# The last sparse tile's values in a buffer of their own, loaded about 15 ticks earlier

## The chip, the cores and the metric

One core of one Trainium2 chip runs the whole program. The metric is the device time of one execution in microseconds; the kernel before took 523.57 us (median of 3 runs, 522.68 to 530.19).

## The reference

Block-sparse attention over 4 batches, 8 heads, 768 positions, head size 64, in blocks of 32; its output rows (3072 tokens of 512 numbers) go through a mixture of 8 experts, of which each token uses one. All in float32.

```python
scores = scale * np.matmul(q, k.transpose(0, 1, 3, 2))
mask = np.abs(blk_i - blk_j) <= window            # window = 1
mask = mask | (blk_i == 0) | (blk_j == 0) | (blk_i == n_blocks - 1) | (blk_j == n_blocks - 1)
for qb in range(n_blocks):
    for kb in sampled_blocks[qb]:                 # 3 sampled blocks for each query block
        mask[qb * block:(qb + 1) * block, kb * block:(kb + 1) * block] = True
attn = softmax(np.where(mask, scores, -1e9)); x = np.matmul(attn, v)
e_idx = np.argmax(x @ w_gate + modality_bias[modality_id], axis=1)
h = np.maximum(x[e_idx == e] @ w1[e], 0.0)        # w1[e]: 512 x 1024, w2[e]: 1024 x 512
out[e_idx == e] = gate_w * (h @ w2[e])
```

## The kernel before, in words

**Attention.** The first and last query blocks attend to everything (dense items). The other 22 blocks of each half of the batch go two at a time: a sparse tile `g` of 22 (`2 * NM`; 11 in each half, `g = half * NM + m`) holds 128 rows. Its keys lie in `kbuf[g % 2]` and its values in `vbuf[g % 2]`, a tile of 128 partitions x 3 columns x 1024: column 1 holds the blocks that both query blocks use (first and last block, put there once in each half's first two tiles and left, and two neighbours), columns 0 and 2 those that one of the two uses alone. `fetch_v` (L509) loads two row blocks of column 1 or 2 (2 DMAs of 128 KB; 4 more where the half begins), `share_v` (L531) copies two row blocks from the tile before on POOL, `fetch_own` (L548) loads the sampled blocks (3 DMAs of 128 KB in each of two calls). All loads are issued from SP's queue, in program order.

**Ticks.** There are 104 items (`NI`): 16 dense ones and 88 sparse ones, four to a tile. The order of the work on every engine is written out: at tick `t` each operation `op` of `ORDER` is done for item `t - LAG[kind][op]`: S scores, M mask and maximum, X exponentials, T transposes (L590), A copies (L595), W `weigh_shared` (L612, products with column 1), V `sum_rows` and `weigh_own` (L605, L621, products with columns 0 and 2), O division, Y transposes of the rows (L628), G gate (L638). Between operations, `hook(place)` runs what `side(t, f, place)` has put there. Tile 19's last item is at tick 95, tile 20's at 99, tile 21's (the last) at 103. W of tile 20 is at tick 104 and V at 106; W of tile 21 at 108 and V at 110. By `VL` and `VG`, tile 19's values are loaded at ticks 95, 96 and 97, tile 20's at 99, 100 and 101, tile 21's at 103, 104 and 105.

**The start of the experts.** `early_groups` (L859) is stepped once a tick, and twice from tick 104 on, beside the end of the attention. It begins at tick 91, so its own count `tick` is 0 there, 12 at tick 103, 19 and 20 at tick 107, 21 and 22 at 108, 23 and 24 at 109. With each of its steps `load` issues half a weight fetch (256 KB, L749) or one `split`: a cast of 128x1024 weights on ACT (L760), whose remainder `low` (L763) is taken on the next step on DVE. `TICKS` (6, 9, 12) says from which count the first, second and third split are due. `staged` gives the first eight weight tiles two staging buffers in turn (a third for the last of them), so weight tile n+2 is fetched after split n. `rows(0)` gathers the token rows of the first expert group (2 indirect DMAs on POOL, L774) once `share_v` of the last tile is issued; 9 steps later `columns(0)` transposes them (L805, two steps of 4 transposes) and casts them (ACT L811, DVE L812). From tick 111 (`tail[0]`) the first products `up` (L818 to L820) of group 0 follow, then `down` (L833 to L835), then group 1, and after the attention's end groups in a loop. Group 1's rows are gathered once `tail[1]` is set, into slot 8, which is the buffer of the odd tiles' values.

**Buffers.** `slot(n)` allocates one of ten tiles; a new allocation of the same slot waits for the last reader of the old one. Slots 0 to 3 and 9 hold dense keys and values, 5 and 6 `kbuf`, 7 and 8 `vbuf`. `expert_slots` takes slots over for the experts: slot 0 (the first batch's keys) and 2 for weights at tick 111.

Of the kernel before, what the change touches and what calls it, by code (L numbers as in the profile page):

```python
# [10 lines left out]
F32R = mybir.dt.float32r  # L11
# [28 lines left out]
NM = NB // 2 - 1  # L40
# [29 lines left out]
VL = (8, 1)  # L70
VS = (11, 7)
VS_SOON = (8, 7)
VG = ((9, 6), (10, 3))

DENSE_IN = ((19, 14, 30), (49, 38, 44))
Q_IN = 22
# [4 lines left out]
EVAC_DVE = ()  # L81
POOL_SPLITS = (7, 15, 16, 21)

TICKS = (6, 9, 12)
DOWN0 = ((9, 5), (9, 7), (14, 7), (12, 9), (13, 9), (13, 9), (17, 9), (15, 10))
UP1 = ((13, 8), (13, 14), (17, 15), (20, 15))
DOWN1 = ((16, 17), (17, 16), (17, 17), (23, 18), (21, 17), (23, 18), (23, 19), (22, 19))
# [3 lines left out]
def attention_moe(ctx, tc, kD, qD, qH, v0, v1, blocks, modality, w_gate, bias, w1, w2, out):  # L91
# [30 lines left out]
    with ExitStack() as actx:  # L122
# [9 lines left out]
        def slot(n, dt=F32):  # L132
            return big.tile([P, 3 * 1024 + 2], dt, name="slot", tag=f"slot{n}", bufs=1)
# [5 lines left out]
        ad = [ad[:, 768 * n:768 * n + 768].rearrange("p (k f) -> p k f", k=6) for n in range(4)]  # L139
        kbuf = [slot(5 + n)[:, 0:3072].rearrange("p (s f) -> p s f", s=12) for n in range(2)]  # L140
        vbuf = [slot(7 + n)[:, 0:3072].rearrange("p (c f) -> p c f", c=3) for n in range(2)]
        qd = {}

        def fetch_q(half, m):
# [363 lines left out]

        def fetch_v(m, half):  # L509
            i, g = 2 * m + 1, half * NM + m  # L510
            vg = vbuf[g % 2]

            def rows_in(r, c, j):
                nc.sync.dma_start(vg[r, c, :].rearrange("p (b f) -> p b f", b=HB), vblock(half, j))

            if m < 2:
                for n, j in ((0, 0), (1, NB - 1)):
                    rows_in(slice(32 + 32 * n, 64 + 32 * n), 1, j)
            if m == 0:
                for n in range(2):  # L520
                    rows_in(slice(0, 32), 1 + n, i + 2 * n)
                for n in range(2):
                    rows_in(slice(96, P), n, i - 1 + 2 * n)
                return
            rows_in(slice(0, 32), 2, i + 2)
            rows_in(slice(96, P), 1, i + 1)
# [4 lines left out]
        def share_v(m, half):  # L531
            g = half * NM + m
            shared.append(g)
            new, old = vbuf[g % 2], vbuf[(g - 1) % 2]
            for r, c in ((slice(96, P), 0), (slice(0, 32), 1)):
                nc.gpsimd.tensor_scalar(new[r, c, :], old[r, c + 1, :], 1.0, 1.0, ALU.mult, ALU.mult)  # L536
            g = max(picked) + 1
            if g < 2 * NM:
                key_numbers(g)
# [7 lines left out]

        def fetch_own(m, half, n):  # L548
            i, g = 2 * m + 1, half * NM + m
            vg = vbuf[g % 2]  # L550
            for k in ((0, 2, 1), (2, 0, 1))[n]:
                reg = own[g][3 * n + k]
                nc.sync.dma_start(vg[32 * (k + n):32 * (k + n) + 32, 2 * n, :].rearrange("p (b f) -> p b f", b=HB), vblock(half, reg))
# [51 lines left out]
                nc.tensor.matmul(tp[32 * j:32 * j + 32, 0:H], lhsT=fold, rhs=r[:, j], start=True, stop=True, tile_position=(0, 32 * j))  # L605

        def weigh_shared(g, o, a):
            vg = vbuf[g % 2]
            for h in range(H):
                pr, u = divmod(h, 2)  # L610
                for b in range(HB):
                    nc.tensor.matmul(o[64 * b:64 * b + 64, D * h:D * h + D], lhsT=a[b][:, 8 * u + 4 + pr].rearrange("p n q -> p (n q)"),  # L612
                                     rhs=vg[:, 1, b * HD + D * h:b * HD + D * h + D], start=h == 0, stop=False, tile_position=(0, 64 * b))

        def weigh_own(g, o, a):
            vg = vbuf[g % 2]
            for h in range(H):
                pr, u = divmod(h, 2)
                for j in range(4):
                    b, n = divmod(j, 2)  # L620
                    nc.tensor.matmul(o[32 * j:32 * j + 32, D * h:D * h + D], lhsT=a[b][:, 8 * u + pr, n],  # L621
                                     rhs=vg[:, 2 * n, b * HD + D * h:b * HD + D * h + D], start=False, stop=h == H - 1, tile_position=(0, 32 * j))
# [61 lines left out]
        def pieces(n, dt, *sizes):  # L684
            t, k = slot(n, dt), 0
            for size in sizes:
                yield t[:, k:k + size]
                k += size
# [5 lines left out]
        def expert_slots(*ns):  # L694
            cols_ = lambda ap: ap.rearrange("p (c t) -> p c t", t=GT)
            W, X, Y = 1024, HD, HD + 1
            for n in ns:
                if n == 0:
                    w = [*pieces(1, F32R, W, W, W), *pieces(3, F32R, W, W, W)]
                    wh[:], wl[:] = w[0::2], w[1::2]  # L700
                    wx = list(pieces(9, F32R, W, W))
                    xh.append(cols_(wx[0]))
                    xl.append(cols_(wx[1]))
                    a = list(pieces(4, F32, W, W, 2 * Y))
                    stg.extend(a[0:2])
                    rows_in(a[2])
                elif n == 2:
                    w = [*pieces(0, F32R, W, W, W), *pieces(2, F32R, W)]
                    wh.extend(w[0::2])
                    wl.extend(w[1::2])  # L710
                elif n == 5:
                    a = list(pieces(5, F32R, 2 * W, W))
                    hh.append(cols_(a[0]))
                    hl.append(cols_(a[1]))
                elif n == 6:
                    a = list(pieces(6, F32R, W, W, W))
                    hl.append(cols_(a[0]))
                    xh.append(cols_(a[1]))
                    xl.append(cols_(a[2]))
                elif n == 7:  # L720
                    stg.extend(pieces(7, F32, W, W, W))
                elif n == 8:
                    a = list(pieces(8, F32, 2 * Y, X, X, W))
                    rows_in(a[0])
                    og.extend(a[1:3])
                    xq.append(a[3])
# [132 lines left out]
        def early_groups():  # L859
# [39 lines left out]
            while not tail[0]:  # L899
                while lows:  # L900
                    lows.pop()()
                rows(0)
                if now["gather"]:
                    wait += 1
                    if wait > 8:
                        columns(0)
                p = sum(tick >= x for x in TICKS)
                load(p + 2, p, True)
                tick += 1
                yield "tick"  # L910
            while lows:
                lows.pop()()
            expert_slots(2, 5, 6, 7)
            while now["column"] < 2:
                rows(0)
                columns(0)
# [350 lines left out]
        def side(t, f, place=7):  # L1267
            work_at.setdefault((t, place), []).append(f)
# [58 lines left out]
        for g in range(2 * NM):  # L1327
            half, m = divmod(g, NM)
            t = at["s", half, m, 0, 0]
            kl = lambda m=m, half=half: q_load(m, half)  # L1330
            qp = lambda m=m, half=half: share_k(m, half)
            vl = lambda m=m, half=half: fetch_v(m, half)
            vg = [lambda m=m, half=half, n=n: fetch_own(m, half, n) for n in range(2)]
            if g < 2:
                loads.update({f"kl{g}": kl, f"qp{g}": qp, f"vl{g}": vl, "vs1": lambda: share_v(1, 0), **{f"v{n}{g}": vg[n] for n in range(2)}})
                continue
            kt = last(g - 2) + KL[0]
            pt = max(kt, t + QP[0])
            vt = last(g - 2) + VL[0]
            side(kt, kl, KL[1])  # L1340
            side(pt, qp, QP[1])
            side(vt, vl, VL[1])
            if m:
                vs = VS_SOON if g >= 2 * NM - 2 else VS
                side(last(g - 2) + vs[0], lambda m=m, half=half: share_v(m, half), vs[1])
            for n in range(2):
                side(last(g - 2) + VG[n][0], vg[n], VG[n][1])

        st, done = {}, set()

# [68 lines left out]
        with man:  # L1419
# [16 lines left out]
            while t < NI + LAG["s"]["G"] + 1 or fillers or slots_todo or choosers or early:  # L1436
                spot = 0
                for op in ORDER:
                    if op in "TSMAXOW":
                        hook(spot)  # L1440
                        spot += 1
                    for kind in "ds":
                        k = t - LAG[kind][op]
                        if 0 <= k < NI and items[k][0] == kind:
                            do(op, items[k])
                hook(7)
                if t >= NI:
                    tail[0], tail[1] = t >= NI + TAIL, t >= NI + LAG["s"]["V"]
                    for _ in range(2):
                        advance(2)  # L1450
                        while slots_todo:
                            slot_lhs(nc.vector if len(slots_todo) % 2 else nc.gpsimd)
                        step(choosers, 1)
                        step(early, 1)
                t += 1
# [61 lines left out]
```

## Time and profile before

| what | us |
|---|---|
| median of 3 runs (range) | 523.57 (522.68 to 530.19) |
| the profiled execution: its time, its span | 527.1, 525.4 |
| PE busy | 501.7 (95%) |
| DVE busy | 386.4 (74%) |
| ACT busy | 336.0 (64%) |
| POOL busy | 248.1 (47%) |
| mean granted TensorE clock | 0.993 |

The profile is one execution on the core. PE is the matmul engine, PEld its weight loads, DVE, ACT and POOL the vector, scalar and GpSimd engines, SP the engine whose queue issues the loads. Idle time before an instruction stands in square brackets with what seems to have ended it. The clock is a share of 2.4 GHz: 1.00 is that level, 0.50 the lower one of 1.2 GHz.

### The profile page before, as it was taken

Reading aid. Unit: us, or ns where it says so; the run is one execution under the profiler, and the core shown is the slowest. Engines: PE = TensorE matmul, PEld = TensorE weight load, DVE = VectorE, ACT = ScalarE, POOL = GpSimd, SP = SyncE. Lnnn points to the kernel's source line nnn. Section 1 sums busy time; section 2 is a strip of 40 time slices with the busy share of each in tenths; the row PEclk is TensorE's granted clock in tenths of the full one; section 3 lists DMA queues with packets and bytes.
Section 4 is the critical chain, followed back from the end, with each engine's and each line's share of the span. In section 5 each row is a group of like instructions: output and inputs, shape, how many; then the busy total and the mean of one; then the engine's idle time right before and its main releaser. Section 6 shows DMA issues by size and latency. Waiting matters only on the chain.

```text
span 525.4 us, 18967 instructions
## 1 busy us (share of the span) xinstructions
PE 501.7 (95%) x7124; PEld 423.3 (81%) x7124; DVE 386.4 (74%) x1136; ACT 336.0 (64%) x765; POOL 248.1 (47%) x514
## 2 busy tenths in 40 slices
PE   7999989979999999789999999999999999999995
PEld 5677767767877867688898898988989899898984
DVE  6886678676689899756986768676686767768673
ACT  4798877978879889634444556555565555555562
POOL 6789675567458983310455241423224222342423
PEclk9999999999999999979999999999999999999999
DMA  8976997899657778946778797969688786867860
GB/s 295 311 218 200 250 254 207 233 246 258 206 165 200 198 214 248 252 123 226 256 237 298 243 310 265 273 223 307 207 260 249 247 283 201 293 199 260 263 225 24
DMA packets 65143, 123.84 MB, mean 236 GB/s; under 512 B 9745, under 2 KB 17682, under 8 KB 65042
## 3 DMA queue, kind: packets, MB, share of 16 engines
q1 hardware_dynamic: 60784, 108.88, 68.2%
q0 software_dynamic: 4256, 13.65, 7.6%
q8 instruction: 58, 0.95, 0.8%
q14 instruction: 43, 0.35, 0.3%
q10 hardware_dynamic: 2, 0.00, 0.0%
HBM read 105.97 MB, written 12.86 MB: 226 GB/s over the span
## 4 chain that ended last, share of the span: by engine, by line
PE 69%; DMA 13%; DVE 10%; issue 3%; SPq 3%; ACT 1%; POOL 1%; DVEq 0%; POOLq 0%; ACTq 0%
PE bank L818 7%; PE bank L819 7%; PE bank L820 7%; DMA slot<-x_d,gi 7%; PE bank L565 6%; PE bank L590 6%; PE bank L834 6%; PE bank L835 6%; PE bank L833 6%; PE bank L612 4%; PE bank L621 3%; DMA slot<-w 3%; PE bank L451 2%; DMA slot<-v 2%; PE bank L638 2%
## 5 line engine op out<-in xcount | busy, mean ns | idle before, releaser
L763 DVE TENSOR_TENSOR slot<-slot 128x1024 fp32r<-128x1024 f32 x99 | 124.7, 1272 | 62.4 <-ACT slot L760 52.6
L760 ACT CAST slot<-slot 128x1024 fp32r<-128x1024 f32 x104 | 107.1, 1047 | 67.2 <-PE bank L819 45.2
L818 PE MATMUL bank<-slot 128*128 128x256 f32 x384 | 108.5, 283 | 0.0
L820 PE MATMUL bank<-slot 128*128 128x256 f32 x384 | 107.8, 281 | 0.0
L819 PE MATMUL bank<-slot 128*128 128x256 f32 x384 | 107.6, 280 | 0.0
L581 ACT ACTIVATE a<-y,mn 128x256 f32<-128x256 f32 x176 | 88.5, 510 | 7.6 <-DVE mn L573 6.8
L854 POOL DMA_INDIRECT out<-slot,si x20 | 27.4, 1369 | 105.7 <-ACT slot L850 102.7
L834 PE MATMUL bank<-slot 128*128 128x512 f32 x192 | 75.9, 395 | 0.0
L833 PE MATMUL bank<-slot 128*128 128x512 f32 x192 | 75.8, 395 | 0.0
L835 PE MATMUL bank<-slot 128*128 128x512 f32 x192 | 75.7, 394 | 0.0
L818 PEld LDWEIGHTS bank<-slot 128*128 128x128 f32 x384 | 72.4, 188 | 0.7 <-ACT slot L760 0.2
L819 PEld LDWEIGHTS bank<-slot 128*128 128x128 f32 x384 | 72.3, 188 | 0.4
L820 PEld LDWEIGHTS bank<-slot 128*128 128x128 f32 x384 | 72.2, 188 | 0.0
L573 DVE CUSTOM_DVE_ANT_1 y<-bank,smask 128x256 f32<-128x256 f32 x176 | 66.2, 416 | 0.3
L502 POOL COPY slot<-slot 128x128 f32 x264 | 64.0, 296 | 0.0
L536 POOL TENSOR_SCALAR slot<-slot 32x1024 f32<-32x1024 f32 x40 | 41.9, 1047 | 33.1 <-PE bank L621 16.8
L595 ACT COPY at<-bank 128x512 f32<-128x512 f32 x88 | 50.6, 576 | 9.8 <-PE bank L590 9.8
L590 PE MATMUL bank<-ident,a 128*128 128x128 f32 x352 | 52.1, 280 | 2.5 <-DVE rt L459 1.6
L565 PE MATMUL bank<-slot,q_raw 64*32 64x256 f32 x1408 | 48.4, 382 | 0.0
L590 PEld LDWEIGHTS bank<-ident,a 128*128 128x128 f32 x352 | 38.1, 141 | 6.9 <-issue 1.7
L835 PEld LDWEIGHTS bank<-slot 128*128 128x128 f32 x192 | 36.1, 188 | 8.5 <-issue 0.2
L834 PEld LDWEIGHTS bank<-slot 128*128 128x128 f32 x192 | 36.0, 188 | 8.3 <-DVE slot L763 0.4
(307 smaller groups left out, 865.5 us busy)
## 6 DMA issues: line engine op xcount, KB each, us to landing
slot<-w SPq DMA_DIRECT2D x100, 512.0 KB
slot<-v SPq DMA_DIRECT2D x188, 128.0 KB
x_d<-xr SPq DMA_DIRECT2D x22, 256.5 KB
q_raw<-qH SPq DMA_DIRECT2D x22, 256.0 KB
slot<-slot SPq DMA_DIRECT2D x120, 32.0 KB
slot<-kD SPq DMA_DIRECT2D x13, 256.0 KB
slot<-v SPq DMA_DIRECT2D x4, 768.0 KB
slot<-v SPq DMA_DIRECT2D x12, 256.0 KB
```

The lines of the kernel that those rows point to most:

```text
L565: nc.tensor.matmul(sp[u][32 * pr:32 * pr + 32, b * 256:(b + 1) * 256], lhsT=q[r, b * NPAIR + pr, n, :], rhs=kv[r, s0:s0 + 8, b, pr, :], st ...
L573: nc.vector.tensor_tensor_reduce(y[:, u, :].rearrange("p (s f) -> p s f", s=8), sp[u][:, b * 256:(b + 1) * 256].rearrange("p (s f) -> p s ...
L581: nc.scalar.activation(a[:, u, :], y[:, u, :], AF.Exp, bias=mn[:, u:u + 1], scale=-1.0, accum_out=total[:, u:u + 1])
L590: nc.tensor.transpose(tp[:, k:k + P], a[:, u, c * P:(c + 1) * P], ident)
L760: nc.scalar.copy(h, s)
L763: (eng or (nc.gpsimd if n in POOL_SPLITS else nc.vector)).tensor_tensor(l, s, h.bitcast(F32), ALU.subtract)
L818: nc.tensor.matmul(o, lhsT=h[:, fs], rhs=xh[g % 2][:, c, :], start=c == 0 and f % 2 == 0, stop=False)
L819: nc.tensor.matmul(o, lhsT=h[:, fs], rhs=xl[g % 2][:, c, :], start=False, stop=False)
L820: nc.tensor.matmul(o, lhsT=l[:, fs], rhs=xh[g % 2][:, c, :], start=False, stop=c == 3 and f % 2 == 1)
L833: nc.tensor.matmul(o, lhsT=hh[0][:, f, ts_], rhs=h[:, fs], start=f == 0, stop=False)
L834: nc.tensor.matmul(o, lhsT=hh[0][:, f, ts_], rhs=l[:, fs], start=False, stop=False)
L835: nc.tensor.matmul(o, lhsT=hl[f // 4][:, f % 4, ts_], rhs=h[:, fs], start=False, stop=f == 7)
```

## The change

The last tile's values get a tile of their own, `slot(0)`. `fetch_v` of tile 21 therefore also loads the first and the last block (2 DMAs more). Its three load calls move from ticks 103, 104, 105 to 88, 95, 97. `share_v` of tile 21 writes the new tile and reads tile 20's. Slot 0's weight pieces become one (at tick 111), slot 2's become three. The third split moves from count 12 to 19, a fourth is done at count 21 (before: at tick 111) with slot 2 taken over then, and the columns wait 10 steps instead of 8. V of the last tile is done at tick 109, ahead of that tick's Y and of `columns(0)`, where before it came at tick 110 behind both.

```diff
+V_LAST = ((-7, 1), (0, 6), (2, 3))
...
-TICKS = (6, 9, 12)
+TICKS = (6, 9, 19, 21)
...
+        vlast = []
+
+        def values(g):
+            if g < 2 * NM - 1:
+                return vbuf[g % 2]
+            if not vlast:
+                vlast.append(slot(0)[:, 0:3072].rearrange("p (c f) -> p c f", c=3))
+            return vlast[0]
...
-            vg = vbuf[g % 2]
+            vg = values(g)
...
-            if m < 2:
+            if m < 2 or g == 2 * NM - 1:
                 for n, j in ((0, 0), (1, NB - 1)):
                     rows_in(slice(32 + 32 * n, 64 + 32 * n), 1, j)
...
-            new, old = vbuf[g % 2], vbuf[(g - 1) % 2]
+            new, old = values(g), values(g - 1)
...
                 elif n == 2:
-                    w = [*pieces(0, F32R, W, W, W), *pieces(2, F32R, W)]
+                    w = list(pieces(2, F32R, W, W, W))
                     wh.extend(w[0::2])
-                    wl.extend(w[1::2])
+                    wl.append(w[1])
                 elif n == 5:
+                    wl.extend(pieces(0, F32R, W))
...
-                    if wait > 8:
+                    if wait > 10:
                         columns(0)
                 p = sum(tick >= x for x in TICKS)
+                if p == 4 and len(wh) == 3:
+                    expert_slots(2)
                 load(p + 2, p, True)
...
-            expert_slots(2, 5, 6, 7)
+            expert_slots(*([2] if len(wh) == 3 else []), 5, 6, 7)
...
-            side(vt, vl, VL[1])
+            if g == 2 * NM - 1:
+                for (later_, nth), f in zip(V_LAST, (vl, *vg)):
+                    side(last(g - 2) + later_, f, nth)
+                vg = []
+            else:
+                side(vt, vl, VL[1])
...
-            for n in range(2):
-                side(last(g - 2) + VG[n][0], vg[n], VG[n][1])
+            for n, f in enumerate(vg):
+                side(last(g - 2) + VG[n][0], f, VG[n][1])
...
+                    if op == "V" and t == NI + LAG["s"]["W"]:
+                        do(op, items[-1])
```

## Rows read from the trace of the kernel before

**Rows 1.** Windows: PE, PEld, DVE, ACT, POOL busy us (count); clock, DMA share, GB/s.
```profile
190.00:205.00 15.00, 14.45 (x396) 10.94 (x397) 14.37 (x76) 12.66 (x39) 9.28 (x20) 1.00 0.86 239
...
212.00:225.00 13.00, 7.55 (x197) 6.46 (x196) 8.54 (x44) 6.85 (x19) 4.33 (x5) 0.97 0.91 247
225.00:231.00 6.00, 6.00 (x100) 5.38 (x100) 3.07 (x22) 3.31 (x6) 0.00 (x0) 0.50 0.22 77
231.00:300.00 69.00, 68.53 (x498) 61.52 (x498) 54.04 (x121) 32.52 (x43) 27.44 (x22) 1.00 0.72 239
300.00:400.00 100.00, 100.00 (x644) 90.67 (x643) 71.20 (x80) 54.84 (x67) 31.61 (x35) 1.00 0.81 262
```

**Rows 2.** Timeline of PE from 214 us: start, length, instructions, idle before.
```profile
214.32 1.15 PE L612 MATMUL bank<-slot,at 128*64 128x64 f32 x30 [1.36 <-ACT at L595]
...
217.08 1.43 PE L621 MATMUL bank<-slot,at 128*32 128x64 f32 x64
...
221.17 0.71 PE L612 MATMUL bank<-slot,at 128*64 128x64 f32 x17 [1.07 <-POOL lhs L390]
224.90 1.12 PE L612 MATMUL bank<-slot,at 128*64 128x64 f32 x15 [3.02 <-issue]
225.95 1.97 PE L805 MATMUL bank<-ident,slot 128*128 128x128 f32 x8
227.71 1.06 PE L628 MATMUL bank<-ident,xr 128*128 128x128 f32 x4
...
228.83 1.91 PE L621 MATMUL bank<-slot,at 128*32 128x64 f32 x64
230.67 0.52 PE L818 MATMUL bank<-slot 128*128 128x256 f32 x1
...
244.99 0.39 PE L833 MATMUL bank<-slot 128*128 128x512 f32 x1
```

**Rows 3.** Timeline of ACT in the same stretch.
```profile
212.76 1.03 ACT L760 CAST slot<-slot 128x1024 fp32r<-128x1024 f32 x1
213.70 0.57 ACT L595 COPY at<-bank 128x512 f32<-128x512 f32 x1
...
219.57 0.59 ACT L595 COPY at<-bank 128x512 f32<-128x512 f32 x1 [0.71 <-PE bank L590]
227.14 0.59 ACT L811 CAST slot<-bank 128x512 fp32r<-128x512 f32 x1 [6.98 <-PE bank L805]
```

**Rows 4.** Timeline of SP, the issuing of the loads, from 198 us.
```profile
198.66 0.88 SPq L514 DMA_DIRECT2D slot<-v  x2
199.74 3.80 SPq L553 DMA_DIRECT2D slot<-v  x6
...
205.24 1.87 SPq L514 DMA_DIRECT2D slot<-v  x2
...
207.86 3.18 SPq L553 DMA_DIRECT2D slot<-v  x6
...
213.93 0.86 SPq L514 DMA_DIRECT2D slot<-v  x2
214.99 1.48 SPq L553 DMA_DIRECT2D slot<-v  x3
...
218.50 2.87 SPq L553 DMA_DIRECT2D slot<-v  x3
```

**Rows 5.** Timeline of POOL: the last two tiles' copies of shared values.
```profile
204.08 2.17 POOL L536 TENSOR_SCALAR slot<-slot 32x1024 f32<-32x1024 f32 x2 [4.74 <-DMA slot<-v]
211.22 2.16 POOL L536 TENSOR_SCALAR slot<-slot 32x1024 f32<-32x1024 f32 x2 [4.97 <-PE bank L621]
```

**Rows 6.** DMA queues from 222 to 223 us: packets, MB, share of 16 engines.
```profile
q1 hardware_dynamic: 154, 0.27, 97.2%
q8 instruction: 1, 0.02, 7.4%
```

**Rows 7.** DMA issues from 212 to 226 us: KB each, us to landing.
```profile
slot<-x_d,gi_e POOLq DMA_INDIRECT x2, 7.4
```

**Rows 8.** Windows, an earlier stretch in which PE stood still (columns as in rows 1).
```profile
115.00:120.00 5.00, 3.41 (x87) 2.73 (x88) 4.29 (x21) 3.59 (x13) 4.74 (x6) 1.00 0.88 243
```

**Rows 9.** Timeline of DVE: the remainder taken beside the columns' cast.
```profile
227.76 0.69 DVE L812 TENSOR_TENSOR slot<-bank,slot 128x512 fp32r<-128x512 f32 x1 [6.84 <-ACT slot L811]
```

More of the change, by code (lines that the diff above doesn't have):

```diff
@@ L549, in fetch_own @@
             i, g = 2 * m + 1, half * NM + m
-            vg = vbuf[g % 2]
+            vg = values(g)
             for k in ((0, 2, 1), (2, 0, 1))[n]:
@@ L607, in weigh_shared @@
         def weigh_shared(g, o, a):
-            vg = vbuf[g % 2]
+            vg = values(g)
             for h in range(H):
@@ L615, in weigh_own @@
         def weigh_own(g, o, a):
-            vg = vbuf[g % 2]
+            vg = values(g)
             for h in range(H):
```

## The prediction

> **What bounds the kernel now.** I first read the busy time by windows. From 231 us to the end of the steady loop PE is busy almost without a break at the full clock (68.53 of 69 us, then 100 of 100) [rows 1], so a microsecond won before 231 us is kept to the end, and none is to be won behind it. The hole is in the stretch that the change touches: from 212 to 225 us PE works 7.55 of 13 us, and from 225 to 231 us it is busy all the time but at the 1.2 GHz level [rows 1].
>
> The timeline of PE then says what the hole is made of [rows 2]. W of tile 20 waits 1.36 us for an ACT copy. W of tile 21 waits 1.07 us; the view names a POOL `lhs`, which these products don't read. Of what they do read, POOL's copies ended at 213.4 [rows 5], the last ACT copy at 220.16 [rows 3], and the two row blocks were issued on SP at 213.93 [rows 4]; by elimination it is the load, some 6 us in flight. Then comes 3.02 us of "issue" in the middle of a group, after 17 of 32 matmuls, where there is no new operand to wait for. In that time a 16 KB packet of the instruction queue moves, between v and row traffic that takes 97% of the DMA engines [rows 6]; I read it as PE waiting for its program. Behind it the clock is low until the `up` products begin at 230.67.
>
> **Part by part**, in us, against the profiled execution's 527.1 (span 525.4), which is 3.5 above the median of the runs.
>
> A. *The third cast leaves tick 103.* It is 1.03 us of ACT right before the copy that W of tile 20 waits for [rows 3]. Without it that copy starts at 212.76 instead of 213.70: **-0.9** (bounds -1.0 and 0, the latter where the values of tile 20 are late instead, see F). Its new place, tick 107, and the fourth cast's at 108 lie behind the last copy, where ACT stands idle for 6.98 [rows 3], so they cost nothing; nor does the later fetch of the fifth weight tile, whose first use is at 244.99 [rows 2].
>
> B. *The load that W of tile 21 waits for is long done.* The 1.07 goes. Next late is the ACT copy (end 220.16), which is within 0.1 of where PE became free: **-1.0** (bounds -1.1 and 0).
>
> C. *The 3.02 us of issue.* The change takes 8 DMAs of 128 KB (2, 3 and 3) [rows 4], 1.05 MB, out of a stretch that moved 13 us x 247 GB/s = 3.2 MB [rows 1]: a third. The rows gathered for the experts (7.4 us to landing [rows 7]) and half a megabyte of weights remain, the weights later. I take the whole stall as gone: **-3.0** (bounds -3.0 and 0).
>
> The Trainium skill speaks against this reading. *Runtime: NRT & Kernel Launch*, section "Instruction fetch mechanics", says an engine's program comes in 16 KiB blocks over a queue of its own while the block before runs, mostly hidden; *DMA: Bandwidth & Descriptors*, section "Queues, rings and completion order", says each DMA engine goes round its queues packet by packet, so a fetch would not stand behind SP's backlog. The block's size agrees with the row (0.02 MB in one packet); that it is hidden does not. By these rules C and D would be nothing, and the sum +1.3 instead of -4.2; that is the first rival.
>
> D. *The clock.* PE stood idle for most of 220 to 225 before it fell, and worked 6.0 us at 0.50 [rows 1]: at most 3.0 us lost. The same 64 products L621 took 1.91 there against 1.43 at 217 [rows 2], so not every instruction doubled. An earlier stretch with 1.59 us of idle in 5 kept its clock [rows 8]. Without B and C the longest idle should be under 2 us: **-2.5** (bounds -3.0 and 0).
>
> E. *V of the last tile goes ahead of the columns.* The same instructions, so no work is added. But before, L628 and L621 ran between the columns' transposes (end 227.9) and `up` (230.67) [rows 2], which hid the cast (0.59 [rows 3]) and the remainder (0.69 [rows 9]). With both moved ahead, PE has nothing to do after the second four transposes until the first column is ready: 0.59 + 0.69 + about 0.3 of hand-over (an estimate), less 0.6 for the second four transposes: **+1.0** (bounds +0.3 and +1.5).
>
> F. *SP gets 10 DMAs more before tile 20's loads.* Six own loads take 3.80 or 3.18 of SP [rows 4], about 0.55 each; 2 row loads 0.88. So 4 at tick 88 cost 1.8, 3 at tick 95 and 3 at tick 97 together 3.3, 5.1 in all, ahead of tile 20's two row blocks (205.24) and six own blocks (207.86 to 211.04). SP is nearly always issuing here, DMA is at 0.86 [rows 1], and little is absorbed; I take 3.5 as the delay. The load before it (issued 198.66 to 199.54) let POOL go at 204.08 [rows 4, 5], 4.5 after the last issue. So the rows of tile 20 land at about 207.1 + 3.5 + 4 = 214.6, and W of tile 20, free from 213.4 by A, waits about 1.2; the own blocks land at about 211.0 + 3.5 + 4 = 218.5, and V of tile 20, which began at 217.08 [rows 2] and would be free at about 217.3, waits about 1.2, a little less as the load on the engines thins. Together **+2.2** (bounds 0, all absorbed in the DMA share left from tick 88 on, and +5, all of SP's time passed on). Tile 19's loads meet only the first 7 of the 10, 1.5 to 2.5 late; they were issued by 203.54 [rows 4], over 7 before the L621 of tile 19 ended and let POOL go at 211.22 [rows 5], so I count nothing there. POOL's copies of tile 21 then start when tile 20's rows land (214.6 rather than 211.22), and the gathers behind them 3 later; with 7.4 they would land at about 226, but the traffic beside them is thinner. The columns want them at about 225: 0 to +1.4, taken as 0.
>
> G. *Group 1's gather* no longer waits for V of the last tile, as slot 8 is free; its columns were not waited for in the stretch after 231 [rows 1], so nothing. Slot 0 was free since the first half of the attention: nothing.
>
> Sum: -0.9 - 1.0 - 3.0 - 2.5 + 1.0 + 2.2 = **-4.2**. The profiled execution would take 522.9, the median 523.57 - 4.2 = **519.4**.
>
> **Rivals.**
> 1. *The stall stays* (C and D are nothing): PE's program comes no sooner, because the gathers and weights still fill the DMA engines, or because the stall isn't their doing. For it: the gathers are not taken away, only moved. Against it: the fetch sits amid 97% load [rows 6]. Then -0.9 - 1.0 + 1.0 + 2.2 = +1.3, so 524.9; with F at 0, 522.7.
> 2. *SP's queue decides* (slower): the 10 DMAs pass all of their time on, tile 20's V waits for its own blocks until about 222, and PE stands idle there instead, so F is +5 and the clock falls as before: -0.9 - 1.0 - 3.0 + 1.0 + 5.0 = +1.1, so 524.7. It decides from own blocks landing after 221 on. For it: SP without pauses; against it: DMA has a seventh of its time free from 190 to 205 [rows 1].
> 3. *SP absorbs all* (F is 0): -6.4, 517.2; with D at -3.0 and E at +0.3 it is -7.6, 516.0.
>
> **How the numbers follow.** Forecast 0.48, rival 1 0.18, rival 2 0.12, rival 3 0.19, something else 0.03. The range goes from 516.0 to 524.9, with 0.7 to 0.9 more at either end for the distance between neighbouring runs (522.68 and 523.57): 515.1 to 525.8. No case reaches 10.5 us, the 2% that a measurement of this kernel can tell from no change, so both outer chances are for the unforeseen: 0.04 each.
>
> **What would show it.** A: no idle before L612 of tile 20 put down to the copy. B: no wait of W of tile 21. C: no "issue" idle between 212 and 230. D: granted clock 1.00 throughout. E: about 1 us before the first L818, ended by DVE L812. F: SP's L514 of tile 20 near 208.7 and idle before L612 or L621 of tile 20 ended by a load. `up` should begin at about 226.5. The prediction is wrong if `up` begins after 229, or if the time won by then is not there at the end.

## The result and the profile after

The changed kernel took 528.49 us (median of 15 runs, 525.20 to 533.87) beside 525.82 for the kernel before on the same chip (15 runs): a ratio of 1.0064, 95% interval 1.0034 to 1.0093. Forecast was 519.4; the time is above the range, and the sign is wrong. Measured again beside the kernel before, on another chip (a_again3), the ratio was 1.0028 (0.9995 to 1.0060), which is not clear of 1. By these two the change costs 1.5 to 3.4 us. (Ratios leave out runs disturbed by a lower clock.) The profiled execution took 526.53, span 524.8, 2.0 below its median.

Windows of the changed kernel, columns as in [rows 1]:

```profile
190.00:205.00 15.00, 13.79 (x395) 10.86 (x388) 14.01 (x74) 13.35 (x40) 8.38 (x19) 1.00 0.92 251
205.00:212.00 7.00, 5.60 (x139) 4.00 (x137) 6.03 (x34) 5.97 (x19) 0.09 (x1) 1.00 0.79 218
212.00:225.00 13.00, 9.50 (x232) 8.37 (x234) 8.40 (x42) 6.89 (x15) 6.17 (x6) 0.85 0.79 203
225.00:231.00 6.00, 5.20 (x62) 4.21 (x55) 3.36 (x15) 2.71 (x5) 1.69 (x2) 0.75 0.82 248
231.00:300.00 69.00, 68.66 (x495) 61.43 (x494) 53.29 (x125) 31.72 (x42) 25.57 (x20) 1.00 0.70 228
300.00:400.00 100.00, 100.00 (x649) 90.70 (x648) 71.39 (x80) 55.98 (x68) 32.36 (x35) 1.00 0.82 265
```

From 212 to 225 us PE works 2 us more than in [rows 1], yet its clock is lower there (0.85 for 0.97). The low clock was not removed, only spread: by these rows 13 x 0.15 + 6 x 0.25 = 3.5 us at most are lost to it, before 13 x 0.03 + 6 x 0.50 = 3.4 (an estimate, which takes PE as busy throughout). Behind 231 us PE is as full as before, as forecast.

The timeline of PE in the changed kernel; line numbers are 10 or 11 higher than in [rows 2] (L612 is now L622, L621 L631, L628 L638, L805 L816, L818 L829):

```profile
199.11 0.28 PE L631 MATMUL bank<-slot,at 128*32 128x64 f32 x2
200.05 1.09 PE L631 MATMUL bank<-slot,at 128*32 128x64 f32 x62 [0.66 <-DMA slot<-v]
...
208.16 1.22 PE L631 MATMUL bank<-slot,at 128*32 128x64 f32 x64
...
213.72 1.47 PE L622 MATMUL bank<-slot,at 128*64 128x64 f32 x32 [2.51 <-DMA slot<-v]
...
218.04 1.54 PE L631 MATMUL bank<-slot,at 128*32 128x64 f32 x64
...
221.03 0.31 PE L622 MATMUL bank<-slot,at 128*64 128x64 f32 x2
222.24 0.69 PE L622 MATMUL bank<-slot,at 128*64 128x64 f32 x16 [0.90 <-ACT at L605]
223.66 0.68 PE L622 MATMUL bank<-slot,at 128*64 128x64 f32 x14 [0.74 <-issue]
...
224.35 1.65 PE L631 MATMUL bank<-slot,at 128*32 128x64 f32 x51
...
227.65 1.23 PE L816 MATMUL bank<-ident,slot 128*128 128x128 f32 x8
229.18 0.38 PE L829 MATMUL bank<-slot 128*128 128x256 f32 x1 [0.30 <-ACT slot L822]
```

W of tile 20 now waits 2.51 for a load of v, and V of tile 18 (x2, then x62) 0.66. W of tile 21 waits for no load, and its "issue" gap is 0.74 instead of 3.02. V of tile 21 stands ahead of the columns, and `up` begins at 229.18: 1.5 earlier than in [rows 2], not the 4.2 of the forecast, and behind the 229 that was named as a sign of being wrong. Even the 1.5 is not won in this stretch: this execution began tile 18's first scores at 177.44, the one of [rows 2] at 179.79.

The timeline of SP shows what stands ahead of tile 20's rows (L524; [rows 4]: L514):

```profile
177.53 4.40 SPq L524 DMA_DIRECT2D slot<-v  x6
...
197.48 1.31 SPq L524 DMA_DIRECT2D slot<-v  x2
199.08 8.06 SPq L563 DMA_DIRECT2D slot<-v  x12
207.40 0.35 SPq L760 DMA_DIRECT2D slot<-w  x1
207.80 0.43 SPq L1318 DMA_DIRECT2D x_d<-xr  x1
208.34 0.85 SPq L524 DMA_DIRECT2D slot<-v  x2
209.39 0.36 SPq L760 DMA_DIRECT2D slot<-w  x1
209.94 3.57 SPq L563 DMA_DIRECT2D slot<-v  x6
```

Twelve own blocks are issued in one piece, six of tile 19 and six of tile 21; the six alone took 3.80 in [rows 4]. From tile 19's row blocks to tile 20's SP now takes 208.34 - 197.48 = 10.9 us instead of 205.24 - 198.66 = 6.6. POOL's copies of shared values ([rows 5]) wait for row blocks too. Those for tile 21 copy from the rows of tile 20 that W20 waits for, and start at 213.66, W20 at 213.72:

```profile
202.90 2.20 POOL L546 TENSOR_SCALAR slot<-slot 32x1024 f32<-32x1024 f32 x2 [5.92 <-DMA slot<-v]
213.66 2.16 POOL L546 TENSOR_SCALAR slot<-slot 32x1024 f32<-32x1024 f32 x2 [8.56 <-DMA slot<-v]
```

On ACT ([rows 3]) the cast has left the copies, and two casts lie together behind the last of them:

```profile
214.56 0.56 ACT L605 COPY at<-bank 128x512 f32<-128x512 f32 x1
...
221.60 0.59 ACT L605 COPY at<-bank 128x512 f32<-128x512 f32 x1 [2.95 <-PE bank L648]
222.08 2.00 ACT L771 CAST slot<-slot 128x1024 fp32r<-128x1024 f32 x2
```

One execution proves little here: the kernel before reached tile 18's first scores at 179.79 in one execution and at 177.94 in another. So I measure stretches, from the starts in PE's timelines: from tile 18's first scores (S18) to tile 21's, to W of tile 20 (W20), to W21, to about that W's end, to the first `up`. "Loads as before" is the mean of four executions (the kernel before twice, b_casts, b_xr6), "changed" that of four executions of the changed kernel.

| stretch, us | loads as before | changed (each) | forecast | found |
|---|---|---|---|---|
| S18 to S21 | 23.67 | 26.46 (24.7, 27.2, 28.8, 25.1) | 0 | +2.8 |
| S21 to W20 | 9.65 | 12.78 (11.6, 13.5, 11.7, 14.3) | +0.3 | +3.1 |
| W20 to W21 | 7.81 | 7.32 (7.3, 7.4, 7.3, 7.3) | +0.2 | -0.5 |
| W21 | 4.80 | 3.00 (3.2, 4.8, 2.8, 1.3) | -3.0 | -1.8 |
| W21's end to `up` | 4.13 | 4.93 (5.0, 4.8, 4.7, 5.3) | +1.0 | +0.8 |
| sum | 50.06 | 54.50 (51.7, 57.7, 55.3, 53.3) | -1.5 | +4.4 |

D's -2.5 belongs to no one stretch; with -0.2 of rounding between A, B and F it makes up the difference to -4.2. Where W20's own wait falls differs: in three of the four executions with loads as before it comes after its first two products, and so counts to the stretch behind W20; in the changed kernel it comes ahead of all of them. Two of the four executions, taken singly (536.75 and 532.7 us), were slower than the timed runs are as a rule; in the other two the sum is +1.7 and +3.3, about the 1.5 to 3.4 of the ratios.

### The profile page after: what moved, and what is told of

Read it like the earlier page. It is cut to its first block, busy times and chain, and to the rows that moved or that the text cites. A ratio compares the mean times of both kernels' runs of the same rounds, so it can differ in the third digit from the quotient of the medians.

```text
span 524.8 us, 18965 instructions
## 1 busy us (share of the span) xinstructions
PE 503.8 (96%) x7124; PEld 424.2 (81%) x7124; DVE 388.6 (74%) x1136; ACT 336.2 (64%) x765; POOL 250.2 (48%) x514
## 4 chain that ended last, share of the span: by engine, by line
PE 63%; DMA 18%; DVE 10%; SPq 4%; ACT 3%; issue 2%; POOL 0%; DVEq 0%; ACTq 0%; POOLq 0%
PE bank L829 6%; PE bank L830 6%; PE bank L831 6%; PE bank L600 6%; PE bank L575 6%; PE bank L846 6%; PE bank L845 6%; PE bank L844 6%; DMA slot<-v 5%; DMA slot<-x_d,gi 4%; DMA slot<-w 4%; PE bank L622 3%; PE bank L631 3%; DVE slot L774 2%; DMA slot<-kD 2%; PE bank L461 2%
## 5 line engine op out<-in xcount | busy, mean ns | idle before, releaser
L829 PE MATMUL bank<-slot 128*128 128x256 f32 x384 | 108.4, 282 | 0.3 <-ACT slot L822 0.3
L865 POOL DMA_INDIRECT out<-slot,si x20 | 27.4, 1369 | 100.4 <-ACT slot L861 97.3
L829 PEld LDWEIGHTS bank<-slot 128*128 128x128 f32 x384 | 72.3, 188 | 1.0 <-ACT slot L822 0.5
L830 PEld LDWEIGHTS bank<-slot 128*128 128x128 f32 x384 | 72.2, 188 | 1.0 <-DVE slot L823 0.5
L831 PEld LDWEIGHTS bank<-slot 128*128 128x128 f32 x384 | 72.2, 188 | 0.0
L846 PEld LDWEIGHTS bank<-slot 128*128 128x128 f32 x192 | 36.1, 188 | 9.3 <-DVE slot L837 0.8
L794 POOL COPY slot<-slot 32x256 f32<-32x256 f32 x40 | 22.1, 553 | 44.6 <-DMA out<-slot,si 36.5
```

What stands on the lines that cost most here:

```text
L829: nc.tensor.matmul(o, lhsT=h[:, fs], rhs=xh[g % 2][:, c, :], start=c == 0 and f % 2 == 0, stop=False)
L830: nc.tensor.matmul(o, lhsT=h[:, fs], rhs=xl[g % 2][:, c, :], start=False, stop=False)
L831: nc.tensor.matmul(o, lhsT=l[:, fs], rhs=xh[g % 2][:, c, :], start=False, stop=c == 3 and f % 2 == 1)
L846: nc.tensor.matmul(o, lhsT=hl[f // 4][:, f % 4, ts_], rhs=h[:, fs], start=False, stop=f == 7)
```

## The experiments

Ratios are to the kernel before, with the 95% interval; 0.001 is 0.53 us.

**Later loads (a_late_loads).** The changed kernel, with the last tile's loads back at ticks 103 to 105.

```diff
-V_LAST = ((-7, 1), (0, 6), (2, 3))
+V_LAST = ((8, 1), (9, 6), (10, 3))
```

> The changed kernel with the last tile's three load calls put back to ticks 103, 104 and 105 (its own buffer, the two extra loads, the later casts and the earlier V stay). Theory Q (the 10 loads ahead of tile 20's on SP's queue make tile 20's values and the row writes late): the 2.5 us wait of W of tile 20 for a load goes, and with it the slowing; 0.996 to 1.000 of the kernel before. Rival O (the new order of V, columns and casts costs, the loads are harmless): still slower, 1.004 to 1.008, and the wait of W of tile 20 is not what counts.

Measured 1.0040 (1.0006 to 1.0074). S21 to W20 is 10.10, near the old 9.65, so the wait ahead of W20 came with the early loads; W21 waits 2.4 for its load instead. The slowing did not go with the wait, as theory Q had wanted: the ratio lies where rival O had it, and V ahead with late loads has a price of its own (b_v_early, below).

**Ten loads more (b_extra10, b_extra10_xr6).** The kernel before, with ten loads that nothing reads, at the changed kernel's ticks; the second also has a sixth division buffer. The last tile's own loads stay where they were.

```diff
+        side(last(19) - 7, extra_rows, 1)
+        side(last(19), lambda: extra_own(0), 6)
+        side(last(19) + 2, lambda: extra_own(1), 3)
```

> The kernel before with 10 loads added that nobody reads, of the same sizes and at the same places of SP's queue (ticks 88, 95 and 97) as the changed kernel's loads of the last tile, into the free slot 0; its own loads of the last tile stay where they were. Theory Q: slower by 2 to 6 us, 1.004 to 1.012, with W or V of tile 20 waiting for a load in the trace. Rival O: at most 1 us, 0.999 to 1.002.

> The 10 unread loads on the kernel before (1.0079) with 6 row buffers (alone 1.0009). If most of the cost of loads ahead on SP runs over the late row writes and the divisions that wait for them: 1.001 to 1.004. If it runs over tile 20's late values: 1.006 to 1.010.

Measured 1.0079 (1.0046 to 1.0112) and 1.0088 (1.0058 to 1.0118): 4.2 and 4.6 us. S21 to W20 is 12.54 and 11.42. This is step F without the other steps, at twice its price; but as the last tile's own loads still come behind, these kernels move eight loads (1 MB) more than the changed one, so the price may be too high for it. The waits of PE from 185 to 240 us with five buffers (in total, times, longest):

```profile
PE bank L612 <- DVE rexp L599: 2.3, 1, 2.3
PE bank L612 <- ACT at L595: 2.2, 1, 2.2
PE bank L805 <- DMA slot<-x_d,gi_e: 1.5, 1, 1.5
...
PE bank L621 <- DMA slot<-v: 0.6, 1, 0.6
```

**A sixth division buffer (a_xr6, b_xr6).** The division L470 writes `xr`, five buffers in turn; each is free when its rows have landed in `x_d`, and those writes are issued on SP too. In the changed kernel it waits for such a write in all four executions (1.7, 6.2, 5.9 and 3.6 us in all). These kernels have six, two small tables being laid into `lhs` to make room.

```diff
-NAT, NXR = 5, 5
+NAT, NXR = 5, 6
```

> The changed kernel with 6 instead of 5 buffers for the rows of a sparse tile (room made by laying two small early tables into a tile that is filled later), so that a division need not wait for the write to x_d of the tile five before. Theory Q with the late row writes as a main part: the waits of the division before L470 (1.15 and 2.39 us in the changed kernel's trace) go, 1 to 3 us faster than the changed kernel: 0.999 to 1.004 of the kernel before. If only the late values count, or rival O holds: 1.005 to 1.008 as the changed kernel.

> The kernel before with 6 instead of 5 row buffers. In the changed kernel the sixth buffer took the ratio from 1.0064 to 1.0003. If that is because the 10 loads made the row writes late (theory Q), it does next to nothing here: 0.998 to 1.001. If the sixth buffer helps whatever the loads (rival), 0.992 to 0.996.

Measured 1.0003 (0.9969 to 1.0036) and 1.0009 (0.9971 to 1.0048). In a_xr6 the division's waits are gone, but W20 still waits 2.5, and S21 to W20 is 12.27. b_xr6 shows none either; of the two traces of the kernel before one has such a wait (1.1 us, b_again) and one has not.

**Loads far ahead (a_far, b_far).** All ten loads of the last tile at ticks 60, 69 and 77, in the changed kernel, and in one with the old order of V and the old casts.

```diff
-V_LAST = ((-7, 1), (0, 6), (2, 3))
+V_LAST = ((-35, 1), (-26, 7), (-18, 7))
```

> The changed kernel with the last tile's loads far ahead, where SP has pauses: its row blocks at tick 60, its own blocks at ticks 69 and 77 (their block numbers are read at tick 60). Theory Q: tile 20's loads are no later than in the kernel before, so A to D of the prediction come out: 3 to 6 us faster than the kernel before, 0.988 to 0.995. Rival O: no better than the changed kernel, 1.004 to 1.008.

> The kernel before with the last tile's values in slot 0 and all its loads far ahead (ticks 60, 69, 77), and nothing else: the third cast at tick 103, V of the last tile at tick 110 behind the columns, the columns after 8 steps. With the far loads and all of the change's other parts the ratio was 0.9987. Theory O2 (the new order of V, columns and casts costs about 2 us, which hides what the loads win): 0.991 to 0.996, faster than that. Rival G (there is little to win, since the idle time seen in the one profile of the kernel before is not in most executions): 0.997 to 1.001. Rival P (the order and the casts help by about 1 us): 1.000 to 1.003.

Measured 0.9987 (0.9949 to 1.0024) and 1.0006 (0.9974 to 1.0037). S21 to W20 is back at 9.44 and 9.45, S18 to `up` takes 46.4 and 46.3 us instead of 50.1: 3.7 less. But the time is not shown to change, where 0.988 to 0.995 was expected of a_far. In these two executions S18 came 0.8 and 1.9 us later than in the mean of the four with loads as before (177.9), and from `up` to the end took 0.2 and 1.4 longer (295.3), so their spans are 2.6 and 0.6 shorter. Whether the far loads cause the later S18 no run here separates.

**V ahead, alone (b_v_early, b_v_early_xr6).** The kernel before with step E alone; the second with six division buffers.

```diff
-                    if wait > 8:
+                    if wait > 10:
...
+                    if op == "V" and t == NI + LAG["s"]["W"]:
+                        do(op, items[-1])
```

> The kernel before with V of the last tile at tick 109 and the columns after 10 steps, and nothing else: its loads are where they were, so V must wait for the own blocks issued last. Theory O2: 1 to 4 us slower, 1.002 to 1.008, with PE waiting for a load before V and for the cast and the remainder before the first product of the experts. Rival G or P: 0.998 to 1.001.

> The kernel before with the last tile's V ahead of the columns, and with a sixth division buffer. V ahead of the columns alone was 1.0074 with five buffers. If V ahead costs because the division under it is held by a late row write, the sixth buffer takes the loss away: 1.000 to 1.002. If it costs by the order itself, the loss stays: 1.005 to 1.009.

Measured 1.0074 (1.0037 to 1.0111) and 1.0067 (1.0036 to 1.0098): 3.9 and 3.5 us, so not the division. With the loads at their old ticks, V's own blocks come last of all, and now the columns stand behind them: W21's end to `up` takes 5.9 and 7.9 us instead of 4.1. PE's timeline in the second (one line further down than the kernel before):

```profile
222.77 1.58 PE L613 MATMUL bank<-slot,at 128*64 128x64 f32 x32
...
224.36 0.28 PE L622 MATMUL bank<-slot,at 128*32 128x64 f32 x2
227.57 1.93 PE L622 MATMUL bank<-slot,at 128*32 128x64 f32 x62 [2.93 <-DMA slot<-v]
...
230.33 1.91 PE L806 MATMUL bank<-ident,slot 128*128 128x128 f32 x8
232.12 0.58 PE L819 MATMUL bank<-slot 128*128 128x256 f32 x1
```

In [rows 2] the columns (L805) run while V's blocks are under way. In order, they wait with V.

**V back in the changed kernel (a_late_v, a_xr6_late_v).** With five and with six division buffers.

```diff
-                    if wait > 10:
+                    if wait > 8:
...
-                    if op == "V" and t == NI + LAG["s"]["W"]:
-                        do(op, items[-1])
```

> The changed kernel with V of the last tile back at tick 110 and the columns after 8 steps; the early loads, the own buffer and the later casts stay. If the new order costs even where the values are there early (predicted +1.0, two profiles of far loads show 1.6 between W of the last tile and the first product of the experts), it is 1 to 2 us faster than the changed kernel: 1.002 to 1.005. If it costs as much as alone with late loads (1.0074), 0.998 to 1.001. If it costs nothing, 1.005 to 1.008.

> The changed kernel with six division buffers and with the last tile's V back behind the columns. If V ahead of the columns costs only through a late input (the division), taking away both gives no more than taking away one: a ratio of 0.998 to 1.002 to the kernel before. If the order costs by itself, this is 1.5 to 3 us below the kernel with six buffers alone: 0.993 to 0.996.

Measured 0.9992 (0.9962 to 1.0022) and 1.0039 (1.0013 to 1.0066). With 1.0064 and 1.0028 for V ahead and five buffers, and 1.0003 for V ahead and six, neither the order nor the buffer is shown to have an effect of its own: V ahead averages 1.0025, V behind 1.0016. That the order costs some 3.8 us in the changed kernel, which a_late_v alone had suggested, did not hold. What makes these four differ by more than their intervals is open.

**The casts, alone (b_casts).**

```diff
-TICKS = (6, 9, 12)
+TICKS = (6, 9, 19, 21)
```

> The kernel before with the later casts and fetches of weights alone (third split at count 19, fourth at 21, the weight slots of the changed kernel); loads, buffers of the values and the order of V as before. Step A of the prediction: 0.9 us faster, and the fetches of weights leave the crowded stretch too: 0.996 to 0.999. Rival: the later weights are missed by the first products of the experts: 1.001 to 1.005.

Measured 1.0000 (0.9968 to 1.0032): neither the gain of 0.996 to 0.999 nor the rival's loss. In its trace W20's wait for the copy is indeed gone, and W20 to W21 takes 6.35 us, where the other three executions with loads as before have 7.5 to 8.9; the "issue" gap in W21 is 3.40 there.

**Loads spread (c_spread, c_spread_v).** The ten loads singly, every third tick from 60 to 87, six division buffers, the later casts; V behind the columns, and V ahead.

```diff
+                side(LAST_AT, queue_last, 0)
+                for n in range(10):
+                    side(LAST_AT + LAST_STEP * n, lambda: singles.pop(0)(), 7)
```

> A version drawn from the runs so far: own buffer for the last tile, its 10 loads one by one every 3 ticks from tick 60 to 87, V and the columns in the order of the kernel before, the later casts, 6 row buffers. With one load at a time SP takes them up without delay, and what the far loads won (4 us between the last scores and the experts' first product) is kept: 0.990 to 0.996. If the loads cost about as much there as they win later, as b_far's 1.0006 has it: 0.998 to 1.001.

> The kernel with ten single loads spread over ticks 60 to 87 and six division buffers, now with the last tile's V ahead of the columns. With every input of V early, V ahead costs nothing by the first theory: a ratio of 0.997 to 1.001, as the kernel it is made from (0.9985). If the order costs by itself, by the casts that then lie bare behind the columns, 1.003 to 1.007.

Measured 0.9985 (0.9957 to 1.0013) and 1.0006 (0.9968 to 1.0044). No wait of W20 for rows is left (S21 to W20 9.72 and 9.38), and in both the clock from 190 to 231 us stayed at 1.00. The first:

```profile
212.00:225.00 13.00, 12.80 (x308) 11.43 (x309) 10.62 (x57) 8.17 (x20) 3.49 (x4) 1.00 0.62 195
225.00:231.00 6.00, 5.36 (x49) 5.11 (x48) 4.10 (x15) 2.71 (x4) 0.00 (x0) 1.00 0.69 226
```

Here 212 to 225 us is nearly full. c_spread has the lowest ratio of all. It lies below the changed kernel's 1.0064, but its interval overlaps that of 1.0028, and it is not shown to be ahead of the kernel before.

**The same kernels again.** The kernel before (b_again: 525.85 us; its "issue" gap was expected at 2.5 to 3.5 us, or below 1.5, and was 2.1) and the changed one three times (a_again1 536.75, a_again2 532.7, a_again3 with the ratio 1.0028 above).

> The changed kernel again, one more profiled execution. If the order of the last tile's V ahead of the columns costs by way of the division that waits for a late row write, its profile shows again a division waiting for an x_d write of over 0.5 us between tile 20's W and tile 21's V, and the W of tile 20 waiting over 1.5 us for its rows. If those waits were chance of one execution, they are absent here, and the loss has another cause.

> The same as the run before it, a third execution of the changed kernel: W of tile 20 waiting over 1.5 us for rows if the loads ahead on SP's queue are the cause; under 0.5 us if it was chance.

> The changed kernel once more, beside the run before this one on the same chip. If its loss is real and not of one chip, 1.004 to 1.009 again. Its profile is a fourth execution: tile 19's or tile 20's own products, or tile 20's W, wait together over 2 us for loads of v if the ten loads put ahead on SP's queue are the cause; under 1 us in all if not.

W20 waits 2.4, 2.3 and 3.4 us, where F had about 1.2, and V of tiles 17 and 18 waits for own blocks as well. The waits of PE from 185 to 240 us, in a_again1:

```profile
PE bank L622 <- issue: 2.9, 1, 2.9
PE bank L631 <- DMA slot<-v: 2.7, 2, 1.6
PE bank L622 <- DMA slot<-v: 2.4, 1, 2.4
PE bank L622 <- DVE xr L470: 1.3, 1, 1.3
```

in a_again2:

```profile
PE bank L631 <- DMA slot<-v: 4.0, 2, 2.8
PE bank L622 <- DVE mn L583: 2.3, 1, 2.3
PE bank L622 <- issue: 1.4, 1, 1.4
```

and in a_again3:

```profile
PE bank L622 <- DVE ho L1149: 3.4, 1, 3.4
PE bank L631 <- issue: 2.1, 5, 0.6
PE bank L622 <- issue: 0.9, 2, 0.6
...
PE bank L631 <- DMA slot<-v: 0.5, 1, 0.5
```

The same wait of W20 (L622) has three names: a load, `mn`, `ho`. It reads neither of the DVE results. What ended it is the same each time: POOL's copies for tile 21, which read the rows of tile 20 and wait for them, start at 223.04, 220.31 and 219.45, and W20 0.06 to 0.07 us behind them (213.66 and 0.06 in the first execution). These rows were issued 9.9, 10.2 and 11.5 us after tile 19's, where the four executions with loads as before have 5.9 to 7.7.

## Why the prediction was wrong

**F is the step that failed first**, as "I take 3.5 as the delay", W of tile 20 "waits about 1.2" and, of the loads before, "I count nothing there". Ten loads on top of the old ones cost 4.2 and 4.6 us (b_extra10, b_extra10_xr6), not 2.2. Counted from S18, SP issued the rows of tile 20 after 30.9, 34.7, 35.2 and 32.5 us in the changed kernel, and after 24.7 to 27.4 with loads as before: 7.2 later in the mean, twice the 3.5, of which PE's own lateness at S21 is 2.8. Three things were off. From tile 19's rows to tile 20's, with the six loads of ticks 95 and 97 between them, SP took 9.9 to 11.5 us for a mean of 6.9, so 3.0 to 4.6 more, where I had put 3.3 for these six and let a third of all be absorbed. The rows of tile 20 let POOL go 4.5, 5.1, 4.5 and 6.0 us after the end of their issue, where I had put 4. And the four loads of tick 88 go ahead of the own blocks of tiles 17 and 18: V of these tiles waits 0.7, 2.7, 4.0 and 0.5 us, where I looked at tile 19 alone. That V of tile 20 would wait 1.2 was wrong too: no execution of the changed kernel shows such a wait. W20's lateness is thus for the most part in the issuing order: by the same rows the transfers themselves are at most 1.5 us slower than tile 19's 4.5 in [rows 4, 5]. That the rest of the loss comes by the queue too, and not by the traffic, is argued and not shown: the same ten loads spread out, or at ticks 60 to 77, left S21 to W20 at 9.4 to 9.7, but there their traffic was out of the way as well.

**F alone does not account for the miss.** With the loads out of the way (a_far, b_far, c_spread, c_spread_v), F is nothing, and the sum would be rival 3's -6.4 for a_far and c_spread_v, which have all the other steps. The ratios of these four are 0.9985 to 1.0006, so -0.8 to +0.3 us, though S18 to `up` is 3.7 to 5.7 us shorter in their traces. The gains of A to D were read from one execution, and the premise that a microsecond won before 231 us is kept to the end is not borne out by the times: S18 itself came 0.4 us earlier (c_spread) to 6.8 us later (c_spread_v) than with loads as before. What makes it late, and where the gain goes, is open.

**A** gave nothing that can be measured (b_casts 1.0000; 0.9 was 0.0017, inside its interval). The wait for the copy did go, in b_casts as in the changed kernel, but in the latter the next thing late was the rows, as its bound of 0 said.

**B** held: no execution of the changed kernel shows W21 waiting for a load, and the kernel with late loads shows 2.4.

**C** was right in size at most in part, and its cause is not borne out. W21 with its gaps is 1.8 shorter in the mean. The "issue" gap was 3.0, 2.1, 3.4 and 3.65 in the four executions with loads as before, 0.7, 2.9, none and none in the changed kernel: less often, but it can come whole. Nor does it go with the old loads: a_late_loads, b_extra10, b_extra10_xr6 and b_v_early_xr6 had the last tile's loads at their old ticks and no gap in W21. In a_again1 it came, 2.85 long, when the DMA engines had nearly nothing to do. The queues in that gap, from 231.5 to 234.3 us (packets, MB, share of 16 engines):

```profile
q0 software_dynamic: 34, 0.09, 8.8%
q1 hardware_dynamic: 26, 0.05, 4.9%
q8 instruction: 1, 0.02, 2.2%
```

and in b_xr6, from 217.9 to 222 us, a gap of 3.65 amid full engines:

```profile
q1 hardware_dynamic: 641, 1.13, 99.1%
q8 instruction: 1, 0.02, 1.9%
q0 software_dynamic: 8, 0.02, 1.5%
```

One packet of the program moves in either. In the trace it began about 0.5 us after PE stopped in a_again1 and about 1.0 after in b_xr6, took 1.0 and 1.25, and PE went on 1.4 after its end. The same holds for every execution with a gap of 0.7 us or more in the middle of W21, nine in all: PE went on 1.2 to 1.5 us after the end of such a packet. In a_again3, without the gap, a packet moved at 221.57, 5 us before W21 began. So the gap goes with a packet that comes late: in the six gaps of 2.1 us and more it began from 0.5 us before PE stopped (b_again) to 1.0 after, in the three shorter ones 0.8 to 1.6 before. The "97%" of [rows 6] is not needed for it: the gap at full engines is 0.8 us longer than the one at 16%. Why the packet comes early in some executions no run here shows.

The Trainium skill's rule that I had set against C, that each DMA engine goes round its queues packet by packet (*DMA: Bandwidth & Descriptors*, "Queues, rings and completion order"), by which a fetch would not stand behind SP's backlog, agrees with these two gaps, whose packets took 1.0 and 1.25 us. That fetching is mostly hidden (*Runtime: NRT & Kernel Launch*, "Instruction fetch mechanics") does not hold at this place in the program, where 2.1 to 3.65 us lay bare in six of the executions above.

**D** gave nothing: 3.5 us lost to the clock for 3.4, and over the runs that the ratio of a_again3 uses the mean loss, (1 - granted clock) x span, was 4.2 us for 3.8. "Without B and C the longest idle should be under 2 us" failed by F: W20's wait of 2.5 stands ahead of the new low stretch. Where that wait is gone (a_far, c_spread, c_spread_v), the clock stayed at 1.00 from 190 to 231 us, but not in b_far, whose longest wait was 1.4:

```profile
212.00:225.00 13.00, 11.64 (x238) 10.14 (x236) 9.73 (x49) 8.40 (x23) 6.77 (x7) 0.87 0.82 230
```

So an idle under 2 us did not suffice. Over the runs of their ratios the mean loss with the loads out of the way is lower by 1.1 (a_far), 0.7 (b_far), 1.0 (c_spread) and 1.9 us (c_spread_v): the part of D that these kernels show.

**E** came near its size inside the change, +0.8 for +1.0, over four executions; in part that is luck, since the old stretch ran at the low clock in some of them ([rows 1]). Its price holds only with B: alone on the old loads it costs 3.5 to 3.9.

**The sum again**, with what was measured: F +4.4, A 0, B and C -1.8, D 0, E +0.8: +3.4, against 1.5 to 3.4 by the ratios. Of the 7.6 us between this sum and the forecast, F's price is 2.2, B and C are 2.2, D is 2.5 and A 0.9. That the sum lands so near is partly luck. F's 4.4 is from kernels with eight loads more, and a_late_v, which has the early loads, was not slower at all (0.9992). The five ratios with the loads at ticks 88, 95 and 97 (1.0064, 1.0028, 1.0003, 0.9992, 1.0039) average 1.0025, the four with them far ahead 0.9996: by these the early loads cost about 1.5 us beside the rest of the change. Rival 2, the one on the slower side, came nearest, with its mark ("tile 20's V waits for its own blocks until about 222") in the wrong place: the rows of tile 20 and the blocks of tiles 17 and 18. It had a chance of 0.12, and its C of -3.0 kept it at +1.1.

## What to carry to other kernels

A transfer moved to an earlier place in an in-order queue can be paid for by everything queued behind it, from the tick of its first piece on: follow the queue tile by tile and ask of each tile whether its own loads had slack, rather than pricing only the last. Here ten loads more at ticks 88, 95 and 97 cost over 4 us, and the ten moved to ticks 60 to 87, singly or in three lumps, nothing measurable. A wait that is gone from one stretch of a trace is not yet time won: compare the whole span, over many executions. An instruction put ahead of others on an engine that works in order puts its late inputs ahead of them too, so such a step is priced together with the loads it needs.

## What the runs showed of the hardware

- A PE gap that goes with a 16 KB packet of the program lasted 2.85 us with the DMA engines at about 16% (a_again1), and 3.65 at full engines (b_xr6); PE went on 1.2 to 1.5 us after the packet's end in nine executions.
- PE's clock fell in the changed kernel with no idle over 2.51 us in the stretch (0.85 from 212 to 225 us), and in b_far with no wait over 1.4 (0.87); it stayed at 1.00 in c_spread, whose longest wait there was 0.9.
- SP took 3.2 to 3.8 us to issue six loads of 128 KB ([rows 4]), and 8.06 for twelve in the changed kernel.
- Executions of one kernel differ in the same place by more than the change is worth: S18 to `up` took 51.7 to 57.7 us in the four executions of the changed kernel.
